# A gated mix of a long convolution and a token MLP on one core: filter transposed through 16-bit PSUM, more sums by accumulating transfers, gate scalings on ScalarE, the last tile cut 512 and 128, and a new fixed order

## The chip, the core and the metric

The kernel runs on one core of a Trainium2 chip. The metric is the device time of one execution in microseconds (us). In the text PE is TensorE, the matrix engine; PEld is its weight load, which overlaps the matmuls; DVE is VectorE; ACT is ScalarE; POOL is GpSimd; SP is SyncE, which here does nothing but issue transfers. SBUF is the on-chip memory, PSUM the accumulators that TensorE writes to.

## The reference

S = 2048 tokens, D = 640 channels, F = 1536. All inputs and the output are bf16. The random inputs are left out.

```python
def reference(A_q, A_k, A_v, A_shift_k, A_ssm_k, A_ssm_D, B_x, B_w1, B_b1, B_w2, B_b2, gate_w):
    def _A_ref(q, k, v, shift_k, ssm_k, ssm_D):
        ...
        for t in range(ks):                      # ks = 4
            k_shift = k_shift + k_pad[:, t:t + S, :] * shift_k[:, ks - 1 - t][None, None, :]
        kv = k_shift * v
        L = 2 * S
        ...
        y_f = kv_f * kf_f[None, :, :, :]         # rfft of kv and of ssm_k, both padded to L
        y = irfft(y_f)[:, 0, :S, :]
        y = y + kv * ssm_D[None, None, :]
        return q * y
    def _B_ref(x, w1, b1, w2, b2):
        h = _layernorm(x, axis=-1)
        u = jnp.einsum("bsd,sf->bdf", h, w1) + b1
        u = _gelu(u)
        y = jnp.einsum("bdf,fs->bds", u, w2) + b2
        return transpose(y, 0, 2, 1)
    x = A_q
    g = _sigmoid((x * gate_w).sum(-1, keepdims=True))
    a = _A_ref(x, A_k, A_v, A_shift_k, A_ssm_k, A_ssm_D)
    b = _B_ref(x, ...)
    return g * a + (1 - g) * b
```

The output is the gated sum of two branches over the same tokens: a causal convolution as long as the sequence (by a Fourier transform of length 4096), and an MLP that mixes tokens.

## The kernel before

**Branch A.** The Fourier transforms are matmuls with cosine and sine tables, after the sequence has been cut by residues of the token index (four parts `p`, two halves). `FE`, `FN` (made in the kernel with a Sin on ScalarE) and `FO` (loaded) are the forward tables, `GTB` the inverse ones. The filter `ssm` comes in as channels by tokens and has to be turned: `transp` does it with matmuls against an identity, eight of 128x128 for each of five channel blocks `db` and two halves, 80 in all; each eight fill one PSUM slot and are evicted to `wT` (L615 on ScalarE, L616 on VectorE). Before its matmuls `transp` adds `dcol`, a column of ssm_D, to the first column of each block on POOL. `wblock` transforms `wT` to the filter's spectrum W in `C[0]`, `C[1]`; `mixing` combines the parts on VectorE, in steps of 2560 or 5120 elements a partition. The keys `kn` are permuted to `kp` (`k_turn`, an operation that either ScalarE or VectorE does), turned by a transposing transfer to `KT`, and convolved with the four taps as matmuls (`kv`); ScalarE evicts to `ksh`, VectorE multiplies with v. `fwd` and `fwd_even` transform the result to `C[2]`, `C[3]`. `cross` and `product` multiply the spectra: `A0` and `A1` are the two halves of kv's spectrum, `V0` and `V1` those of the filter's. Some of the sums are not done by VectorE but by a transfer that adds to its destination, issued by POOL (L267, accum): so `late` in `product`, and `acc_dma`, which adds V1 to A1 in two transfers of 640 KB each for g = 1 and g = 0. `invmix` and `halved` prepare the inverse, `inverse` does its matmuls against `GTB`; ScalarE scales the result by the gate into `cgb`, VectorE multiplies by q (`q_hi`, `q_lo`: reloaded from the input late, since X's place is taken by then), and the product is added to `O1`, which already holds the MLP's result: for the first half h = 0 by an accumulating transfer, for h = 1 by VectorE.

**Branch B.** X holds the input, `ln_tile` takes mean and variance (two statistics operations of 320 and one that joins them, per tile of 128 tokens), `ln_scale` and `ln_apply` normalize in place. m1: 12 blocks `ft` of 32 matmuls with 320 columns, X against w1 (in `ring`), into one PSUM slot, then gelu on ScalarE into `GT`. m2: 16 tiles (hk, p) of 24 matmuls, GT against w2 (`W2`), evicted by ScalarE with scale and bias to `O1`; the last tile is evicted by two VectorE operations of 320 columns (`last_stt`, L627), which add the convolution's part.

**Gate.** gsum on ScalarE adds up q * gate_w per token; a few operations of 16 elements a partition on VectorE and a tanh make `gg` (g) and `omg` (1 - g).

**PSUM.** Four slots pp0 to pp3, each 128 x 1024 fp32 (two banks). Both branches take their slots from these four.

**The order.** Nothing is scheduled at run time. Every operation is recorded by `SC.add` with what it reads and writes; `follow` then takes a written list of the 649 operations (`_ORDER`), which fixes the order on every engine and every issuing queue, `_SLOTS` fixes the PSUM slot of each group, and `_ENG` the engine of each of the 50 operations that can run on either. `_Tracker` puts in the semaphore waits. Each engine works in the order of its list, so an instruction that waits holds up all behind it. Ahead of the first transposes TensorE runs matmuls on zeros (`spin`, tile `zz`, 512 columns each); they compute nothing. m1's and m2's matmuls stand between those of branch A, so that TensorE has work while VectorE is at the spectra.

In the profile the lines of helpers appear rather than their callers': L298 is every matmul, L556 every two-operand VectorE or POOL operation, L570 to L571 every operation with a scalar, L600 ScalarE's, L636 memsets, L615 and L616 the evictions on either engine, L267 POOL's and L272 SP's transfers.

Of the kernel before, what the change touches and what calls it, by code (L numbers as in the profile page):

```python
# [19 lines left out]
class _Tracker:  # L20
# [265 lines left out]
    def mm(self, ps_ap, lhsT, rhs, start, stop, final_val, inc, transpose=False):  # L286
# [11 lines left out]
        ins = self.nc.tensor.matmul(ps_ap, lhsT=lhsT, rhs=rhs, start=start, stop=stop, skip_group_check=True)  # L298
# [134 lines left out]
def _build(nc, A_q, A_k, A_v, A_shift_k, A_ssm_k, A_ssm_D, B_x, B_w1, B_b1, B_w2, B_b2, gate_w, out):  # L433
# [10 lines left out]
    with ExitStack() as es:  # L444
# [53 lines left out]
        cst = alloc("cst", [128, 2], F32)  # L498
# [27 lines left out]
        ksh = [alloc(f"ksh{i}", [128, 4, D], BF16, at=base_of(GT) + 5120 * (1 + i)) for i in range(2)]  # L526
        rows = alloc("rows", [20, 5, 512], BF16, at=base_of(GT))
# [110 lines left out]
        def mms(vt, items, prio=None, name="mm"):  # L638
            dur = sum(max(n_of(r) / 2400.0 + 0.0025, 0.056) for _, _, r, _, _ in items)
            rd = []  # L640
            for _, l, r, _, _ in items:
                rd += [l, r]

            def emit(s):
                fv = T.cnt["PE"] + 1
                for k_, (o, l, r, st, sp) in enumerate(items):
                    T.mm(o(s), l, r, st, sp, fv, k_ == len(items) - 1)
            return SC.add("PE", dur, emit, rd, [], prio=prio, vt=vt, name=name)
# [43 lines left out]

        def x_load(hk):
            dma(X[:, hk, :, :], qrow(hk), 128 * 5120, chain=True, rate=(352.0 if hk == 0 else 415.0))
# [28 lines left out]
        ssm_load(0, 0, 1)  # L723
        for a, b in ((0, 1), (1, 4)):
            dma(X[:, 0, a:b, :], dr(A_q, a * D, [[4 * D, 128], [1, (b - a) * D]]), 128 * 1280 * (b - a), chain=True)
        ssm_load(1, 0, 1)
        for db in range(1, ND):
# [3 lines left out]
        for hk in range(1, 4):  # L731
            x_load(hk)
# [14 lines left out]
        memset("DVE", cst[:, 1:2], -0.5)  # L747
        iota = lambda ap, pat, b, cm: nolock("POOL", 0.1 + n_of(ap) / 1100.0, lambda s: T.op("POOL", lambda e: e.iota(ap, pat, base=b, channel_multiplier=cm), [], [ap]), [], [ap])
# [49 lines left out]
        def transp(h, db):  # L798
# [5 lines left out]
            for j in range(7, -1, -1):  # L804
                items.append(((lambda s, j=j: s[:, 128 * j:128 * j + 128]), V(ssm, db * S + 1024 * h + j, [[8, 128]]), ident[:, :], True, True))
            m_ = mms(vt, items, name="wtr")
            evac("wT", V(wT, 2 * h * SL + 128 * db, [[SL, 2], [D, 4], [1, 128]]), (lambda s: s[:, :].rearrange("q (a b c) -> q a b c", a=2, b=4)), vt, 1.0 / 1024.0)
# [93 lines left out]

        def ln_scale(a, b):
# [24 lines left out]
        for h in range(2):  # L927
# [5 lines left out]
            if h == 0:  # L933
# [20 lines left out]
                def stats_of(k):  # L954
                    for t in range(LB[k], LB[k + 1]):
                        b0, b1, ag = ln_tile(t // 4, t % 4)
# [19 lines left out]
                mixing(C[0], SS, 0, fine=True, prio=MIXP)  # L976
# [104 lines left out]
        ts("DVE", gpre[:, :], mv[:, :, 0], gws[:, 0:1], None, ALU.mult, mode=1)  # L1081
        tt("DVE", gpre[:, :], gpre[:, :], gth[:, :], ALU.add, mode=1, prio=0)
        act(gth[:, :], gpre[:, :], ACT.Tanh, scale=0.5, prio=0)
        ts("DVE", gg[:, :], gth[:, :], 0.5, 0.5, ALU.mult, ALU.add, mode=1, prio=0)
        ts("DVE", omg[:, :], gth[:, :], -0.5, 0.5, ALU.mult, ALU.add, mode=1, prio=0)
# [20 lines left out]

        INVP = ((0, 2, 1, 3), (1, 3, 0, 2))
        for hk, p in [(hk, p) for hk in range(2) for p in range(4)] + [(hk, p) for p in INVP[1] for hk in (2, 3)]:
# [7 lines left out]
            for a in range(na):  # L1116
                items = []
                for ft, ci in order[a * (24 // na):(a + 1) * (24 // na)]:
                    items.append((chk(ci), w2t(hk, p, ft), GT[:, ft, 320 * ci:320 * ci + 320], ft == 0, ft == FT - 1))
# [26 lines left out]
        def product(dst, a, v, late=None, into=None):  # L1146
# [14 lines left out]
            tt("DVE", P2(T1), P2(a), P2(v, True), ALU.mult)  # L1161
            tt("DVE", H(dst, 0), H(T0, 0), H(T0, 1), ALU.subtract)
            tt("DVE", H(dst, 1), H(T1, 0), H(T1, 1), ALU.add)
# [32 lines left out]
        def invmix(Ya, Yb, sc, bfirst=False, behind=None):  # L1196
# [8 lines left out]
            for (hy, sy), k in (((hb, sb), 1), ((ha, sa), 0)) if bfirst else (((ha, sa), 0), ((hb, sb), 1)):  # L1205
# [29 lines left out]
        def inverse(h, Z, G=None):  # L1235
            for p in INVP[h]:
# [24 lines left out]
                tt("DVE", qv if h == 0 else cg[:, :, :], cg[:, :, :], qv, ALU.mult)  # L1261
                if h == 1 and p == INVP[1][-1]:
# [4 lines left out]
                    for ci in range(2):  # L1267
                        last_stt(O1[:, 3, p, 320 * ci:320 * ci + 320], chk(ci), omg[:, t:t + 1], cg[:, 1, 320 * ci:320 * ci + 320], lastvt[ci])
                    dma(rows_of(1, p, 1, 1), O1[:, 3, p, :], 128 * 1280, sem="out")
                elif h == 0:  # L1270
                    dma(ov, qv, 128 * 2560, stream="POOL", prio=0, accum=True)
                    dma(rows_of(0, p, 0, 2), ov, 256 * 1280, sem="out")
# [19 lines left out]
        chained(product, A1[1], A1[1], V0[1], tmp_of(q_hi, 0), V1[1])  # L1292
        chained(product, A1[0], A1[0], V0[0], tmp_of(q_hi, 1), V1[0])
        acc_dma(A1[1], V1[1])
        acc_dma(A1[0], V1[0])
        chained(product, A0[1], A0[1], V0[1], H(V0[1], 0))
        lastacc = SC.ops[-1]
        assert lastacc.eng == "POOL"
        for kt in range(2):
            dma(q_hi[:, kt, :, :], qrow(kt), 128 * 5120, wait=[H(A0[1], 1)]).deps.add(lastacc)  # L1300
        chained(product, A0[0], A0[0], V0[0])
        for kt in range(2):
            dma(q_lo[:, kt, :, :], qrow(2 + kt), 128 * 5120)
# [15 lines left out]
13 1 24 20 26 41 6 0 55 23 29 31 28 21 2 30 32 25 22 7 53 27 51 33 10 34 11 57 35 14 42 36 59 17 37 8 52 56 12 39 40 4  # L1319
48 44 142 54 136 9 49 50 145 43 135 203 3 67 233 137 5 139 68 204 60 138 58 144 61 18 69 141 209 74 140 62 182 75 210  # L1320
207 146 76 65 208 183 143 79 160 66 166 163 72 80 156 81 157 147 211 184 73 159 162 82 161 158 212 164 124 95 63 118
96 123 83 181 215 165 70 120 64 117 100 84 216 167 119 148 121 213 107 85 187 150 205 71 104 188 151 114 88 89 168 122
101 206 169 77 115 102 103 90 86 125 116 185 126 214 91 105 98 171 127 97 87 186 219 106 99 108 92 172 174 93 129 78
109 220 110 221 178 197 222 94 149 130 217 112 236 113 198 19 133 225 179 237 218 131 45 223 267 191 111 235 226 46
199 224 155 128 201 132 170 134 200 192 382 202 255 234 176 153 173 264 177 256 387 189 265 262 152 240 260 154 190
241 383 263 242 388 175 193 261 389 180 194 243 257 384 258 266 253 390 254 196 274 244 391 272 385 238 259 275 239
273 366 386 195 268 247 270 269 367 246 227 271 278 280 279 282 368 281 283 276 284 316 277 245 47 228 313 317 311 314
318 312 309 319 285 320 369 286 310 321 301 230 370 287 297 302 299 288 229 289 300 295 290 322 293 249 296 401 298
250 315 294 291 329 292 327 231 402 330 328 333 325 232 334 331 403 332 326 303 252 323 335 337 336 404 251 338 348
324 372 405 340 38 341 373 397 342 371 339 398 346 16 304 343 374 347 344 349 352 345 356 353 452 377 375 357 354 400  # L1330
376 306 406 380 381 350 305 399 15 421 379 351 307 422 378 355 423 308 424 392 407 360 395 416 425 408 358 396 361 393
417 533 394 359 418 411 419 459 461 538 409 415 420 446 460 532 412 447 414 413 448 426 441 442 535 428 458 248 430
443 534 410 436 429 537 427 536 449 444 431 539 432 451 363 541 437 453 438 540 454 450 445 474 456 457 362 433 455
# [36 lines left out]
```

## Time and profile before

| what | value |
|---|---|
| median of 3 runs | 177.09 us (176.99 to 177.10) |
| the profiled execution | 177.12 us |
| its span, first to last instruction | 175.1 us |
| mean granted TensorE clock | 1.00 |
| moved by transfers | 44.06 MB, mean 252 GB/s |

Where each engine is busy over the span shows in 40 equal slices (a digit is the busy share in tenths, 9 means 90% or more; PEclk is the granted clock; DMA the share of the 16 transfer engines):

```profile
PE   7999999999899999999999999999999999999992
PEld 2599999877697767777777778888899998698782
DVE  7899999999999999999999999999999999999984
ACT  4499999997999997877556214222215105645760
POOL 3199891000000650003202202220055000052200
PEclk9999999999999999999999999999999999999999
DMA  5999999999999799992999999999939999549598
```

The costliest groups of instructions (busy time, mean ns of one, idle time before them and what ended it) that the change touches:

```profile
L556 DVE TENSOR_TENSOR C<-C 128x2560 bf16<-128x2560 bf16 (+2 forms) x38 | 54.6, 1485 | 0.3 <-ACT C L600 0.2
...
L267 POOL DMA_DIRECT2D C<-C x8 | 10.5, 1674 | 51.1 <-DVE C L556 30.0
...
L600 ACT ACTIVATE gq<-gq 128x640 bf16<-128x640 bf16 x16 | 11.6, 727 | 5.7 <-DVE gq L556 5.7
L556 DVE TENSOR_TENSOR tm<-C,C 128x5120 bf16<-128x5120 bf16 x5 | 14.1, 2819 | 0.1
L897 DVE BATCH_NORM_STATS2 stats<-X 128x6 f32<-128x320 bf16 x32 | 13.1, 470 | 0.4 <-DMA X<-in_A_q_dram 0.2
```

A group's busy time is not its price. Each VectorE product of 2560 lasts 1.48 us but the next starts 1.40 us after it, and a matmul of 320 columns lasts 299 ns while the next starts 136 ns after it: times from start to start add up, durations don't.

### The profile page before, as it was taken

The page shows a single profiled execution, that of the slowest core. Times are in us where ns is not written, and L with a number is a line of the kernel's source. Part 1 is how long each engine was busy: PE and PEld are TensorE (multiplying, and loading weights), DVE is VectorE, ACT ScalarE, POOL GpSimd, SP SyncE. Part 2 cuts the span into 40 slices and gives each one's busy share as a digit, 9 for nine tenths or more (in the row PEclk, how much of TensorE's full clock was granted, in tenths as well). Part 3 has the DMA queues.
Part 4 walks back from the last instruction along what each step waited for, and adds up shares of the span by engine and source line. Part 5 has one row for each costly group of instructions (what it writes and reads, how often), then busy time and mean ns, then how long its engine had stood idle before and what let it go on. Part 6 is the DMA issues. An engine that isn't in the chain of part 4 may idle for free.

```text
span 175.1 us, 3683 instructions
## 1 busy us (share of the span) xinstructions
PE 170.0 (97%) x1559; PEld 138.2 (79%) x1559; DVE 168.9 (96%) x187; ACT 107.6 (61%) x160; POOL 42.7 (24%) x62
## 2 busy tenths in 40 slices
PE   7999999999899999999999999999999999999992
PEld 2599999877697767777777778888899998698782
DVE  7899999999999999999999999999999999999984
ACT  4499999997999997877556214222215105645760
POOL 3199891000000650003202202220055000052200
PEclk9999999999999999999999999999999999999999
DMA  5999999999999799992999999999939999549598
GB/s 144 397 421 405 376 200 225 380 375 221 179 383 356 172 192 192 186 358 57 178 174 365 353 211 349 282 207 240 300 108 187 197 177 372 241 65 209 106 233 292
DMA packets 33248, 44.06 MB, mean 252 GB/s; under 512 B 12112, under 2 KB 24656, under 8 KB 33104
## 3 DMA queue, kind: packets, MB, share of 16 engines
q1 hardware_dynamic: 28024, 32.68, 57.6%
q0 software_dynamic: 5168, 11.14, 37.4%
q8 instruction: 12, 0.20, 0.4%
q14 instruction: 4, 0.03, 0.1%
q10 hardware_dynamic: 40, 0.01, 0.0%
HBM read 27.44 MB, written 2.62 MB: 172 GB/s over the span
## 4 chain that ended last, share of the span: by engine, by line
PE 93%; DMA 3%; ACT 2%; DVE 0%; DVEq 0%; SPq 0%; issue 0%
PE pp L298 93%; DMA ssm<-in_A_ssm_k_dram 3%; ACT L600 1%; ACT ksh L600 1%; ACT GT L600 0%; DVE O L627 0%; DVEq L426 0%; SPq L272 0%
## 5 line engine op out<-in xcount | busy, mean ns | idle before, releaser
L298 PE MATMUL pp<-X,ring 128*128 128x320 bf16 x384 | 55.4, 299 | 0.5 <-ACT GT L600 0.5
L556 DVE TENSOR_TENSOR C<-C 128x2560 bf16<-128x2560 bf16 (+2 forms) x38 | 54.6, 1485 | 0.3 <-ACT C L600 0.2
L298 PE MATMUL pp<-GT,W 128*128 128x320 bf16 x384 | 53.6, 299 | 0.0
L298 PEld LDWEIGHTS pp<-GT,W 128*128 128x128 bf16 x384 | 48.0, 129 | 4.6
L298 PEld LDWEIGHTS pp<-X,ring 128*128 128x128 bf16 x384 | 37.0, 98 | 15.0 <-ACT GT L600 0.8
L600 ACT ACTIVATE O<-pp,c,omg 128x640 bf16<-128x640 f32 x15 | 12.9, 883 | 24.8 <-PE pp L298 24.8
L267 POOL DMA_DIRECT2D C<-C x8 | 10.5, 1674 | 51.1 <-DVE C L556 30.0
L600 ACT ACTIVATE C<-pp 128x640 bf16<-128x640 f32 x32 | 20.4, 711 | 2.0 <-PE pp L298 2.0
L600 ACT ACTIVATE cgb<-pp,gg 128x640 bf16<-128x640 f32 x16 | 12.1, 795 | 13.3 <-PE pp L298 7.6
L615 ACT ACTIVATE C<-pp 128x1024 bf16<-128x1024 f32 x18 | 17.1, 1051 | 0.3 <-PE pp L298 0.3
L600 ACT ACTIVATE gq<-gq 128x640 bf16<-128x640 bf16 x16 | 11.6, 727 | 5.7 <-DVE gq L556 5.7
L556 DVE TENSOR_TENSOR tm<-C,C 128x5120 bf16<-128x5120 bf16 x5 | 14.1, 2819 | 0.1
L897 DVE BATCH_NORM_STATS2 stats<-X 128x6 f32<-128x320 bf16 x32 | 13.1, 470 | 0.4 <-DMA X<-in_A_q_dram 0.2
L298 PE MATMUL pp<-wT,FO 128*128 128x128 bf16 x160 | 12.4, 219 | 0.0
L600 ACT ACTIVATE GT<-pp,cc 128x640 bf16<-128x640 f32 x12 | 9.3, 793 | 4.8 <-PE pp L298 4.7
L298 PE MATMUL pp<-C,GTB 128*128 128x320 bf16 x80 | 11.9, 299 | 0.0
L298 PE MATMUL pp<-wT,FE 128*128 128x128 bf16 x120 | 11.7, 219 | 0.0
L556 DVE TENSOR_TENSOR SS<-C 128x2560 bf16<-128x2560 bf16 x8 | 11.7, 1482 | 0.0
L267 POOL DMA_DIRECT2D O<-q_hi x4 | 4.8, 1324 | 27.7 <-DVE q_hi L556 27.7
L600 ACT ACTIVATE ksh<-pp 128x1024 bf16<-128x1024 f32 (+1 forms) x12 | 10.1, 908 | 1.4 <-PE pp L298 1.3
L267 POOL DMA_DIRECT2D C<-q_hi x4 | 4.8, 1198 | 23.8 <-DVE q_hi L556 10.9
L556 DVE TENSOR_TENSOR C<-tm 128x2560 bf16<-128x2560 bf16 x7 | 10.3, 1487 | 0.1
(92 smaller groups left out, 225.3 us busy)
## 6 DMA issues: line engine op xcount, KB each, us to landing
ring<-in_B_w_dram SPq DMA_DIRECT2D x12, 512.0 KB, 8.8
W<-in_B_w_dram SPq DMA_DIRECT2D x12, 512.0 KB, 6.8
C<-C POOLq DMA_DIRECT2D x8, 640.0 KB, 8.8
kn<-in_A_k_dram SPq DMA_DIRECT2D x4, 640.0 KB, 9.6
C<-q_hi POOLq DMA_DIRECT2D x4, 640.0 KB, 9.7
out_dram<-O SPq DMA_DIRECT2D x7, 320.0 KB, 3.2
ssm<-in_A_ssm_k_dram SPq DMA_DIRECT2D x4, 512.0 KB, 7.0
X<-in_A_q_dram SPq DMA_DIRECT2D x3, 640.0 KB, 7.3
```

What stands on the lines that cost most here:

```text
L267: ins = engobj.dma_start(out_ap, in_ap, accum_op=ALU.add, max_dma_last_dim=2560)
L298: ins = self.nc.tensor.matmul(ps_ap, lhsT=lhsT, rhs=rhs, start=start, stop=stop, skip_group_check=True)
L556: o_ = SC.add(eng, d, lambda s: T.op(eng, lambda e: e.tensor_tensor(o, a, b, op), rd, [o]), rd, [o], prio=prio, name="tt")
L600: return T.op("ACT", lambda e: e.activation(o, src, func, **kw), rr + [src], ww)
L615: return either(name, o, i, [], lambda e, src: e.activation(o, src, ACT.Copy, **kw), lambda e, src: e.tensor_copy(o, src) if scale == 1.0 ...
L897: ops.append(SC.add("DVE", 0.38, (lambda o, i: lambda s: T.op("DVE", lambda e: e.bn_stats(o, i), [i], [o]))(o, i), [i], [o]))
```

## The change

- `T.mm` gets `is_transpose`; `transp` sets it and writes bf16 into PSUM, so that eight transposes fill half a slot. The evictions to `wT` read bf16.
- `cst` gets a fourth column that holds 0.5 (a memset on POOL). The gate's `gpre`, `omg` and `gg` are made by ScalarE instead of VectorE.
- The statistics of tile 11 are made by ScalarE (`ln_tile_act`: two passes over the tile with a running sum, and a tiny one between them).
- `mixing(C[0], ...)` takes its first steps 5120 wide, and `invmix` too where its two halves lie side by side.
- `product` loses the form with three operations on VectorE: both A0 products now add one part by an accumulating transfer. They come ahead of the A1 products, and each A1 product is followed by its own pair of `acc_dma`. The loads of `q_hi` lose a wait that held them until a sum had been issued.
- In `inverse` the second half's parts p = 1 and p = 3 are added to `O1` by an accumulating transfer instead of VectorE.
- The last m2 tile and its two evictions are cut at column 512 instead of 320; each piece has its own output transfer.
- Loads: block 4 of ssm and part 1 of X come first, in two pieces each (before, block 0 and part 0); FO, GTB and the small loads change places.
- `_ORDER`, `_SLOTS` and `_ENG` are new. In the new list the first 40 transposes stand back to back; all 14 matmuls on zeros are ahead of them (before, 12 ahead and two between). The 1.28 us load of ScalarE's gelu table stands behind the Sin at the start (before, ahead of the first gelu). 16 + 16 matmuls of m1 stand ahead of the first of `kv` (before 8 + 8). One of the four `kp` copies is on ScalarE, and seven wT evictions instead of eight.

```diff
-        ins = self.nc.tensor.matmul(ps_ap, lhsT=lhsT, rhs=rhs, start=start, stop=stop, skip_group_check=True)
+        ins = self.nc.tensor.matmul(ps_ap, lhsT=lhsT, rhs=rhs, start=start, stop=stop, skip_group_check=True, **({"is_transpose": True} if transpose else {}))
...
+        junk = alloc("junk", [128, D], BF16, at=base_of(GT) + 10240)
...
-        ssm_load(0, 0, 1)
+        ssm_load(0, 4, 5)
         for a, b in ((0, 1), (1, 4)):
-            dma(X[:, 0, a:b, :], dr(A_q, a * D, [[4 * D, 128], [1, (b - a) * D]]), 128 * 1280 * (b - a), chain=True)
-        ssm_load(1, 0, 1)
-        for db in range(1, ND):
+            dma(X[:, 1, a:b, :], xpart(1, a, b), 128 * 1280 * (b - a), chain=True)
+        ssm_load(1, 4, 5)
+        for db in [d for d in range(ND) if d != 4]:
...
+        memset("POOL", cst[:, NCST:NCST + 1], 0.5)
...
-                items.append(((lambda s, j=j: s[:, 128 * j:128 * j + 128]), V(ssm, db * S + 1024 * h + j, [[8, 128]]), ident[:, :], True, True))
-            m_ = mms(vt, items, name="wtr")
+                items.append(((lambda s, j=j: s[:, 64 * j:64 * j + 64].bitcast(BF16)), V(ssm, db * S + 1024 * h + j, [[8, 128]]), ident[:, :], True, True))
+            m_ = mms(vt, items, name="wtr", transpose=True)
...
+        def ln_tile_act(t):
+            xs = X[:, t // 4, t % 4, :]
+            r = 1.0 / math.sqrt(D)
+            act(junk[:, :], xs, ACT.Copy, scale=1.0 / D, acc=mv[:, t, 0:1], name="lnm")
+            act(cst[:, 2:3], mv[:, t, 0:1], ACT.Copy, scale=-r, name="lnb")
+            act(junk[:, :], xs, ACT.Square, scale=r, bias=cst[:, 2:3], acc=mv[:, t, 1:2], name="lnm")
...
-                mixing(C[0], SS, 0, fine=True, prio=MIXP)
+                mixing(C[0], SS, 0, prio=MIXP)
...
-        ts("DVE", gpre[:, :], mv[:, :, 0], gws[:, 0:1], None, ALU.mult, mode=1)
+        act(gpre[:, :], mv[:, :, 0], ACT.Copy, scale=gws[:, 0:1])
...
+        LASTC = (0, 512, 640)
...
-            tt("DVE", P2(T1), P2(a), P2(v, True), ALU.mult)
-            tt("DVE", H(dst, 0), H(T0, 0), H(T0, 1), ALU.subtract)
-            tt("DVE", H(dst, 1), H(T1, 0), H(T1, 1), ALU.add)
...
+            if ha is hb and sb + 2 == sa:
+                y0, y1 = (V(ha, (sb + j) * SL, [[2 * SL, 2], [1, SL]]) for j in range(2))
+                tt("DVE", V(hs, (ss + 1) * SL, [[-SL, 2], [1, SL]]), y0, y1, ALU.add)
+                tt("DVE", y0, y0, y1, ALU.subtract)
...
-                tt("DVE", qv if h == 0 else cg[:, :, :], cg[:, :, :], qv, ALU.mult)
+                by_dma = h == 0 or p in (1, 3)
+                tt("DVE", qv if by_dma else cg[:, :, :], cg[:, :, :], qv, ALU.mult)
...
-        chained(product, A1[1], A1[1], V0[1], tmp_of(q_hi, 0), V1[1])
-        chained(product, A1[0], A1[0], V0[0], tmp_of(q_hi, 1), V1[0])
-        acc_dma(A1[1], V1[1])
-        acc_dma(A1[0], V1[0])
-        chained(product, A0[1], A0[1], V0[1], H(V0[1], 0))
-        lastacc = SC.ops[-1]
-        assert lastacc.eng == "POOL"
-        for kt in range(2):
-            dma(q_hi[:, kt, :, :], qrow(kt), 128 * 5120, wait=[H(A0[1], 1)]).deps.add(lastacc)
-        chained(product, A0[0], A0[0], V0[0])
-        for kt in range(2):
-            dma(q_lo[:, kt, :, :], qrow(2 + kt), 128 * 5120)
+        for g in range(2):
+            chained(product, A0[g], A0[g], V0[g], tmp_of(tm[1], g))
+        for g in (1, 0):
+            chained(product, A1[g], A1[g], V0[g], tmp_of(q_hi, g), V1[g])
+            acc_dma(A1[g], V1[g])
+        for hk in range(2):
+            dma(q_hi[:, hk, :, :], qrow(hk), 128 * 5120)
+        for hk in range(2):
+            dma(q_lo[:, hk, :, :], qrow(2 + hk), 128 * 5120)
```

`_ORDER`, `_SLOTS` and `_ENG` are replaced as a whole and not shown.

## Prediction

> **What bounds the kernel now.** I read the busy shares and slices first, then the chain of waits, then the timeline at the chain's joints, then the transfers at the end.
>
> ```profile
> PE 170.0 (97%) x1559; PEld 138.2 (79%) x1559; DVE 168.9 (96%) x187; ACT 107.6 (61%) x160; POOL 42.7 (24%) x62
> ...
> PE 93%; DMA 3%; ACT 2%; DVE 0%; DVEq 0%; SPq 0%; issue 0%
> ```
>
> TensorE (PE) and VectorE (DVE) are both full. Being full is not yet being the bound; the chain in order of time says which one ends last:
>
> ```profile
> 1.19 5.37 DMA ssm<-in_A_ssm_k_dram
> 6.56 0.04 issue
> 6.60 27.17 PE pp L298 x443
> ...
> 41.09 1.02 ACT ksh L600
> 42.11 0.02 issue
> 42.13 1.28 ACT L600
> 43.41 0.01 issue
> 43.43 0.81 ACT GT L600
> 44.23 0.05 issue
> 44.28 127.63 PE pp L298 x988
> ...
> 171.93 0.55 DVE O L627
> 172.48 0.46 DVEq L426
> ```
>
> TensorE works from 6.60 to 171.91 and stops once for long: from 43.61, when the matmuls before it are done, until 44.28 it waits for the first gelu, which stood behind a 1.28 us reload of ScalarE's function table. All other idle places of TensorE after 6.60 come to about 0.6 us, and 0.43 us goes into two idle-spin matmuls on zeros at 7.65. So an edit that leaves the columns alone can gain some 1.2 to 1.7 us, no more. Two other resources are close behind:
>
> ```profile
> 15.00:20.00 5.00, 5.00 (x91) 5.00 (x89) 4.94 (x15) 5.00 (x8) 4.66 (x7) 1.00 1.03 405
> 20.00:25.00 5.00, 5.00 (x91) 4.97 (x90) 5.00 (x16) 5.00 (x7) 4.39 (x9) 1.00 1.26 246
> ```
>
> (busy PE, PEld, DVE, ACT, POOL of 5 us; clock; DMA share; GB/s.) ScalarE (ACT) has no room either from 15 to 25 us, and the DMA share is at 1.
>
> **The change, part by part.** The sum starts from the profiled execution, 177.12 us, of which 175.1 is its span and 2.0 lies around it; the median of the runs shown is 177.09, so the two agree.
>
> (a) *Head, to the first W matmul* (9.60 in before). The Pool engine (POOL) now makes three jrow tables (0.19 us each) ahead of brow, and memsets (0.36 for rows, 0.15 for m32) stand ahead of pint on DVE: pint ends 0.75 later and with it the 1.15 us Sin. Behind Sin ScalarE now does the table load (1.28) and a statistics pass over tile 11 (0.73, priced by a gsum row of the same 128x640), and only then dcol, for which the addition to ssm and so the transposes wait: 7.7 against 5.93, about 0.35 us of stall on TensorE after 6.6. A second pass (0.73), cw (0.28) and cc are ahead of the first wT eviction, so it ends at 10.07. Two spins fewer (0.43) give some of it back. First W matmul at 10.1: **+0.5**. If fillers hide it, 0; if each late step adds, +1.1.
>
> (b) *Table load gone from 42.13*: the gelu follows the ksh eviction at once. Its cover before was nothing, TensorE stood: **-0.67**.
>
> (c) *16-bit transposes.* The 80 matmuls keep their 128 columns (56 ns from start to start); I take no change. The evictions' bounds: on DVE 1.18, as now, to 0.43 (the row of an int16 1024-wide pass); on ScalarE 1.04 in both. Three of ten are on DVE, none is on TensorE's path once W runs: 0, range -0.3 to +0.3.
>
> The Trainium skill, "VectorE: DVE Perf Modes", section "Why PSUM operands drop a tier", says a PSUM operand in 16 bits may run at twice the rate that one in fp32 gets. By it the DVE eviction would be an estimated 0.6 us, and the sum would not change.
>
> (d) *ScalarE +3.3 us of work before 40 us*: a 128x2560 kp copy (2.4 by the slope of the 727 and 1051 ns rows, 2.9 by that to the 1149 one), two 0.73+0.19 passes, small ones; one eviction goes to DVE. Where ScalarE is full its followers, the slots' evictions, come later by up to that. The cover is the m1 filler matmuls put ahead of the k convolution, 32 x 0.136 = 4.35 us: 0 taken; without cover, up to +2. DVE loses 5.4 us (seven 2560-wide products at 1.40, three more 5120-wide at 2.74, two 1280-wide, three statistics, one kp copy, plus one eviction), mostly after 100 us, where TensorE is fed through other work: no gain by itself.
>
> (e) *The products and the accumulating transfers.* In before:
>
> ```profile
> 128.87 1.20 POOL L267 DMA_DIRECT2D C<-SS  x1 [10.41 <-DVE C L556]
> 129.60 4.17 POOL L267 DMA_DIRECT2D C<-C  x3
> ...
> 147.13 2.89 DVE L556 TENSOR_TENSOR SS<-C 128x2560 bf16<-128x2560 bf16 x2
> ...
> 164.12 4.51 PE L298 MATMUL pp<-SS,GTB 128*128 128x320 bf16 x32
> 168.47 3.42 PE L298 MATMUL pp<-GT,W 128*128 128x320 bf16 x24
> ```
>
> The four sums (issued 0.73 apart) land 6.2, 8.7, 11.3 and 14.9 us after issue by the rows of the transfers, so at 135.1, 138.3, 141.6 and 146.0: 3.2, 3.3 and 4.4 us apart. Afterwards the A0 products come first and the sums into A1 in two pairs. The first pair's DVE work ends where it does now, 128.9; the second follows one 5120-wide and four 2560-wide operations, 2.74 + 4 x 1.40, at 137.4. Ahead of and between them are two W loads (1.5 us each) and, no longer held back by a wait, two q_hi loads (1.7 each): 128.9 + 4 x 3.3 + 3.0 + 3.4 = 148.5 for the last landing. DVE waits for it with SS<-C, and behind that stand the rest of the inverse mixing and all that TensorE's last inverse needs: two 5120-wide and four 2560-wide, 11.5 us with the hand-overs. Then TensorE has 64 matmuls at 0.136 and the last tile, 12.2 with the start. So TensorE would end at 148.5 + 11.5 + 12.2 = 172.2, against 171.91 - 0.67 + 0.5 = 171.74 if nothing made it wait. The later decides; I take **172.1**, +0.2. The bounds: if the last lands as early as in before, 171.74 (-0.2); at 4.4 us for each of the four it is 172.2 + 4.4 = 176.6 (+4.7), but three of four in before were not so slow, so I value the step near its lower end.
>
> (f) *The end.* Twelve 512-wide matmuls (0.216) and twelve 128-wide (0.056) are 3.26 us, as 24 x 0.136 was. The last DVE operations, 128 and 512 wide, sum to the same 1.0 us. But two O1 sums of 320 KB go by transfer (4.1 us alone, by an O<-q_hi row), so one output of 320 KB starts at about 171 instead of before, and the outputs already land one per 0.92 us:
>
> ```profile
> out_dram<-O SPq DMA_DIRECT2D x1, 320.0 KB, 2.6
> out_dram<-O SPq DMA_DIRECT2D x1, 160.0 KB, 1.8
> ```
>
> Two of 320 KB and then 32 and 128 KB behind 172.1 are 2.3 us of backlog and 0.5 us of issue: the last lands near 175.2 instead of 174.8. **+0.2** on top of TensorE's end. If the sums land earlier, 0; if the backlog is whole, +0.8.
>
> (g) Load order, gate scalings (three tiny ones, 0.17 to 0.22 us each), the larger mixing steps: hidden behind TensorE's filler; exposed they cost up to 0.3.
>
> Sum: 177.12 + 0.2 (TensorE's end, which holds a to e) + 0.2 (f) = **177.5**. This kernel's measurement can tell some 0.2% (0.35 us) from no change.
>
> **The rivals.**
>
> *Faster.* The head's lateness is met by other matmuls and the sums land by 147 as now, for the q_hi loads are small and the two pairs compete less than four at once. For it: TensorE's slack in the filler stage, and that (b) is a stall surely removed. Against it: DMA share 1 and the longer way from the sums to the end. It gives -0.67 + 0.2 + 0 = 176.65, and with the two spins and half of the small gaps gone too, 176.1. It decides wherever the last sum lands before 148.
>
> *Sums late* (slower). The last sum takes 4.4 us, as the last in before, because loads share the engines: 149.6, and the end 173.3, 1.2 over what I took: 178.7; both of the second pair so slow, 179.8. For it: the fourth sum of before. Against it: the first three.
>
> *Transposes slow TensorE.* The change puts 40 transposes back to back, with no zero spins between, from 6.7 to about 10. If they do not keep the clock up, columns cost 0.427 us per 512 as in the first spins (ten took 4.30) in place of 0.216: 40 transposes from 2.24 to 4.5 us, +2.2: 179.7. For it: TensorE does start slow in before, ten spins at 0.43. Against it: the same 40 ran at 56 ns in before, with two spins of zeros among them.
>
> The Trainium skill, "TensorE: Matmul & The Clock Gate", section "Part 4: PE-mode transpose", says this mode does not count as TensorE being busy for the clock. Here the 80 were ordinary matmuls against an identity and become such ones, and no run of this case shows the mode yet; by the rule the time is this rival's.
>
> *It doesn't do what it says.* A 16-bit eviction takes as long as a 32-bit one. Then (c) is 0 exactly and 177.5 stays.
>
> **Chances.** Forecast, with its own range 176.9 to 178.1: 0.43, of which 0.14 falls within 0.2% (up to 177.44) and 0.29 above. Faster rival 0.34 (0.32 below 176.74, 0.02 within). Sums late 0.14, transposes 0.06, no effect of 16 bits 0.03 (within 0.01, above 0.02). That gives faster 0.32, same 0.17, slower 0.51. The range leaves out a tenth on each side: from 176.1, where the faster rival has everything, to 179.0, past the late sums.
>
> **What would show it.** First W matmul near 10.1, and dcol near 7.7 (a). A table load near 5.5 and none at 42; the gap at 43.6 gone (b). Transposes 56 ns apart at clock 1.00, DVE evictions from 16 bits below 1.18 (c). No TensorE idle time on ACT from 15 to 40 (d). The 5120-wide SS<-C waiting for a DMA until about 148.5, and TensorE waiting for DVE behind it (e): if TensorE shows no gap there, (e) is wrong and the time falls below 177. Outputs landing to 175.2 (f). A clock below 1 before 15 us, or TensorE gaps at the k convolution, would make the whole forecast wrong upward.

## The result, and the profile after

The changed kernel takes 186.83 us (median) against 177.04 us before: 1.0526 times as long, with a 95% interval of 1.0469 to 1.0584. One of its four executions, 189.61 us, fell in a slower state and is left out of the ratio, which compares the means of the others. The prediction was 177.5 us with a range up to 179.0. The sign was right, the size was not: 9.8 us were lost where 0.4 were forecast.

The profiled execution took 186.81 us with a span of 185.3. First the slices of its page, 40 equal parts of that span (4.6 us each), a digit being tenths of busy time and, for PEclk, tenths of TensorE's full clock:

```profile
PE   7999999999999609999999999999999999999990
...
PEclk9999999999999985899999999999999999999998
...
DMA  6999999999999999178589898998999998996796
```

In the 14th and 15th slice, from about 60 to 70 us, TensorE is idle, and for the two slices behind that its clock is down. The rest of TensorE's row looks as in the kernel before. The 20 us from 60 on held 150 matmuls in the kernel before and hold 83 now (before, then after: length, busy PE, PEld, DVE, ACT, POOL with instructions, granted clock, DMA share, GB/s):

```profile
60.00:80.00 20.00, 20.00 (x150) 14.25 (x148) 19.76 (x15) 16.12 (x31) 2.42 (x2) 1.00 1.06 227
```

```profile
60.00:80.00 20.00, 13.95 (x83) 8.87 (x82) 11.15 (x8) 9.18 (x16) 2.42 (x2) 0.83 0.83 174
```

The stretches of 20 us from 80 to 140 hold as many as before, 149 or 150 each. The loss is one event, not a slow-down of the whole. The waits of TensorE and the chain of work name it:

```profile
PE pp L298 <- DMA ring<-in_B_w_dram: 6.0, 1, 6.0
PE pp L298 <- DVE cst L638: 1.2, 1, 1.2
PE pp L298 <- DMA ssm<-in_A_ssm_k_dram: 0.2, 1, 0.2
```

```profile
50.16 0.55 SPq L272
50.71 0.04 issue
50.75 0.67 SPq L272
51.42 0.04 issue
51.47 17.73 DMA ring<-in_B_w_dram
69.19 0.04 issue
69.24 7.10 PE pp L298 x30
```

(In order of time: start, length, what.) TensorE waits once for 6.05 us, from 63.2 to 69.24, for the last of the four 512 KB pieces of w1 that go to the second ring buffer. SP issues this piece at 51.47 and it takes 17.73 us to land. What SP issued just ahead of it, and what landed late, stand in SP's timeline and in the list of transfers issued in that stretch (KB each, us to landing):

```profile
50.16 0.55 SPq L272 DMA_DIRECT2D ring<-in_B_w_dram  x1
50.75 0.67 SPq L272 DMA_DIRECT2D GTB<-inv_tab  x1
51.47 0.74 SPq L272 DMA_DIRECT2D ring<-in_B_w_dram  x1
...
GTB<-inv_tab SPq DMA_DIRECT2D x1, 1024.0 KB, 12.2
ring<-in_B_w_dram SPq DMA_DIRECT2D x1, 512.0 KB, 17.7
```

The 1 MB table GTB, needed for the first inverse at 149 us and not before, is now loaded ahead of a piece that TensorE needs at 63.2. In the kernel before, GTB was issued at 90.07, between the W loads, and the last ring piece landed 10.2 us after its issue:

```profile
ring<-in_B_w_dram SPq DMA_DIRECT2D x1, 512.0 KB, 10.2
```

GTB's own transfer is some 2.5 us: in the experiment below that holds the sums back, it lands 2.5 us behind the piece ahead of it (61.98 against 59.44). That alone would not make 17.7. The rest shows in the queues of the transfer engines, packets and share of 16 engines, in the windows 61 to 63 and 67 to 69 us. q1 carries SP's loads, q0 what POOL issues, here the first accumulating sums:

```profile
q0 software_dynamic: 121, 0.31, 81.1%
q1 hardware_dynamic: 171, 0.17, 28.3%
...
q0 software_dynamic: 171, 0.41, 108.2%
q1 hardware_dynamic: 13, 0.01, 2.2%
```

Two sums of 640 KB were issued at 56.62 and 57.62 and begin to move at about 60.5, when 363 of the ring piece's 512 packets of 1 KB are still to come. From then on the sums take most of the engines' time: between 67 and 69 us, 11 of the piece's packets go through (q1's other two have 4 bytes). Of the sixteen parts of the piece, one on each engine, the first has landed at 60.98, fourteen by 65.06, and the last two at 68.54 and 69.19.

The wait is not all that it costs. The windows before, in and behind it (busy PE, PEld, DVE, ACT, POOL with instructions, then the granted clock, DMA share, GB/s):

```profile
57.00:63.20 6.20, 6.19 (x46) 3.87 (x43) 6.20 (x5) 5.60 (x10) 4.56 (x4) 1.00 1.07 347
63.20:69.20 6.00, 0.00 (x0) 0.00 (x0) 5.05 (x3) 1.38 (x3) 0.16 (x1) 0.92 1.09 211
69.20:71.70 2.50, 2.46 (x10) 1.42 (x11) 0.00 (x0) 0.00 (x0) 0.00 (x0) 0.50 1.09 207
71.70:74.20 2.50, 2.50 (x11) 1.42 (x10) 0.00 (x0) 2.08 (x5) 0.00 (x0) 0.50 0.97 183
74.20:76.70 2.50, 2.50 (x17) 1.63 (x15) 0.00 (x0) 1.26 (x4) 0.00 (x0) 0.83 0.17 32
```

TensorE comes back at half its clock: 10 matmuls in 2.5 us instead of 18. PE's busy column is full there, so only the counts and the clock show it. The mean clock of the wait, 0.92, puts the fall to a half some 5 us into it, and the 0.83 of the last window puts the return at about 75.1. That is 5.8 us of work at half the clock, up to 2.9 us lost.

The Trainium skill, "TensorE: Matmul & The Clock Gate", section "HAM oscillation — how this bites in real kernels", describes this: a wait for a transfer longer than about 3.4 us takes TensorE's clock down to a half, and it starts again from there. The trace agrees: 6.05 us of standing still gave 0.50, and in an experiment below 1.66 us gave 1.00. Where between the two the limit lies, no run here shows.

### The profile page after: what moved, and what is told of

Its sections match the earlier page's. It is cut to its first block, busy times and chain, and to the rows that moved or that the text cites. A ratio compares the mean times of both kernels' runs of the same rounds, so it can differ in the third digit from the quotient of the medians.

```text
span 185.3 us, 3685 instructions
## 1 busy us (share of the span) xinstructions
PE 173.4 (94%) x1558; PEld 138.2 (75%) x1559; DVE 163.6 (88%) x175; ACT 111.6 (60%) x168; POOL 48.1 (26%) x66
## 4 chain that ended last, share of the span: by engine, by line
DVE 43%; DMA 21%; ACT 13%; PE 11%; SPq 6%; issue 3%; POOL 0%; DVEq 0%
DVE C L558 23%; PE pp L298 11%; DMA ring<-in_B_w_dram 10%; DVE tm L558 9%; DMA ssm<-in_A_ssm_k_dram 6%; SPq L272 6%; DMA C<-C 5%; ACT C L617 5%; DVE q_hi L558 3%; DVE SS L558 3%; DVE gq L558 3%; ACT ksh L602 3%; ACT X L930 2%; ACT kp L712 1%; ACT wT L617 1%
## 5 line engine op out<-in xcount | busy, mean ns | idle before, releaser
L298 PE MATMUL pp<-X,ring 128*128 128x320 bf16 x384 | 57.7, 307 | 6.0 <-DMA ring<-in_B_w_dram 6.0
L298 PEld LDWEIGHTS pp<-X,ring 128*128 128x128 bf16 x384 | 38.0, 100 | 21.9 <-DMA ring<-in_B_w_dram 6.4
L298 PE MATMUL pp<-GT,W 128*128 128x320 bf16 (+2 forms) x383 | 53.0, 299 | 0.1
L298 PEld LDWEIGHTS pp<-GT,W 128*128 128x128 bf16 x384 | 47.2, 129 | 5.4
L602 ACT ACTIVATE C<-pp 128x640 bf16<-128x640 f32 x32 | 21.0, 707 | 11.4 <-PE pp L298 9.7
L267 POOL DMA_DIRECT2D C<-C x8 | 9.9, 1415 | 67.2 <-DVE C L558 67.2
L602 ACT ACTIVATE gq<-gq 128x640 bf16<-128x640 bf16 x16 | 11.6, 724 | 11.5 <-DVE gq L558 11.5
L558 DVE TENSOR_TENSOR tm<-C,C 128x5120 bf16<-128x5120 bf16 (+1 forms) x5 | 12.7, 2553 | 0.0
L558 DVE TENSOR_TENSOR SS<-C 128x2560 bf16<-128x2560 bf16 (+1 forms) x6 | 11.4, 1931 | 0.2
L602 ACT ACTIVATE ksh<-pp 128x1024 bf16<-128x1024 f32 (+1 forms) x12 | 10.3, 914 | 0.5 <-PE pp L298 0.5
L298 PEld LDWEIGHTS pp<-C,GTB 128*128 128x128 bf16 x80 | 7.7, 98 | 3.0
L298 PEld LDWEIGHTS pp<-wT,FO 128*128 128x128 bf16 x160 | 9.8, 98 | 0.0
```

Of the source, the lines that this page charges most:

```text
L267: ins = engobj.dma_start(out_ap, in_ap, accum_op=ALU.add, max_dma_last_dim=2560)
L558: o_ = SC.add(eng, d, lambda s: T.op(eng, lambda e: e.tensor_tensor(o, a, b, op), rd, [o]), rd, [o], prio=prio, name="tt")
L602: return T.op("ACT", lambda e: e.activation(o, src, func, **kw), rr + [src], ww)
```

## The experiments

The theory (A): GTB's place on SP's queue put the last ring piece into the stretch in which the accumulating sums run, and these stretched it. Rival (B): the sums slow the piece wherever GTB stands. Rival (C): something else of the change is what counts. The edits to the order are moves of one number in the written list; operation numbers are those of the recorded list.

### GTB right behind the ring piece, and GTB where it was

```diff
 _ORDER (after; 247 is GTB, 246 the last ring piece)
-... 276 312 247 317 313 310 318 246 285 ...
+... 276 312 317 313 310 318 246 247 285 ...
```

> The changed kernel with one thing moved: the 1 MB GTB load stands right behind the last ring piece on SP's queue instead of right ahead of it. Theory A (GTB pushed the ring piece by 3.8 us, into the accumulating sums, which then stretched it): the piece lands near 61, before TensorE asks for it at 63.2, the 6.05 us wait and the half-speed stretch behind it are gone, and the time falls by about 8.7 us to 178.1. Rival B (the accumulating sums slow the piece wherever it stands): it lands at 65 or later, TensorE still waits 2 us or more, 181 or slower.

Measured: 178.20 us, ratio to the kernel before 1.0063 (1.0038 to 1.0089). The piece, by the list of transfers:

```profile
GTB<-inv_tab SPq DMA_DIRECT2D x1, 1024.0 KB, 12.9
ring<-in_B_w_dram SPq DMA_DIRECT2D x1, 512.0 KB, 10.4
```

It lands at 60.87, before it is needed, and TensorE no longer waits for it. 8.6 of the 9.8 us hang on the place of one load. B falls, for the sums are issued at nearly the same time as in the changed kernel (56.92 against 56.62); C falls for these 8.6 us.

```diff
 _ORDER (after)
-... 276 312 247 317 ... 533 458 435 ...
+... 276 312 317 ... 533 458 247 435 ...
```

> The changed kernel with the GTB load where the kernel before has it, between the W loads. Theory A: no wait for the ring, and the sums no longer share the engines with GTB either, 177.5 to 178.1 (what is left of the change beside the load order, forecast at 177.5). Rival B: 181 or slower, as in the run with GTB right behind the ring. If both runs end above 180 with no wait for the ring, something else in the change costs the time.

Measured: 179.99 us, ratio 1.0146 (1.0109 to 1.0182). No wait for the ring, but slower than with GTB behind the ring, which was not expected. The transfers give one reason: GTB now lands at 98.6, and the sums and W loads behind it land later (a q_hi sum issued at 90.04 takes 11.68 us, where it took 6.91; the C<-C sum issued about 97 takes 9.37 instead of 6.42). VectorE then waits 1.3 us for that sum, and TensorE, at the inverse transforms from 144 us on, waits three times for VectorE, 0.3 to 0.55 us each. These waits are 1.35 us, where the run with GTB behind the ring has 0.39. They are not the whole: in this profile, of the slowest of the four executions (180.95 us), TensorE ends 2.6 us later than there, and 1.0 of that are longer waits for the filter in the first 21 us, which GTB's place doesn't explain. In this order an early GTB is right in itself; it stood one place too early.

### GTB early in the kernel before

```diff
 _ORDER (before; 248 is GTB, 245 its last ring piece)
-... 284 316 277 245 47 228 ... 428 458 248 430 ...
+... 284 316 277 248 245 47 228 ... 428 458 430 ...
```

> The kernel before with one thing moved: GTB right ahead of its last ring piece. Theory A: that piece, needed at 60.3, lands at 63 or later, up to 69 if the sums stretch it; TensorE waits 3 to 9 us and then runs slow for a while: 181 to 187. Rival B (GTB is harmless, the sums decide): within 1 us of 177.04.

Measured: 178.50 us, ratio 1.0079 (1.0052 to 1.0106): slower, but not by the 4 to 10 us of the expectation. Its timeline and its clock:

```profile
61.86 1.26 PE L298 MATMUL pp<-X,ring 128*128 128x320 bf16 x8 [1.66 <-DMA ring<-in_B_w_dram]
```

```profile
61.80:64.30 2.50, 2.44 (x18) 1.78 (x19) 2.47 (x2) 0.87 (x2) 1.28 (x2) 1.00 1.08 203
```

The piece lands at 61.82 there, 11.0 us after its issue: GTB pushed it by some 2.5 us, but the sums, issued 0.8 us later than in the changed kernel (57.43), began to move at 60.69, when 22 of its 512 packets were left, against 363 in the changed kernel. So there GTB costs a wait of 1.66 us and no clock. The expensive part is the meeting with the sums, and about a microsecond decides whether they meet.

### The sums wait until the piece is there

```diff
-                    128 * 5120, stream="POOL", prio=0, accum=True)
+                    128 * 5120, stream="POOL", prio=0, accum=True, wait=[ring[1][:, 12:16, :]])
```

(in `v1mix` of the changed kernel, GTB left in its early place)

> The changed kernel, GTB where the change puts it, but the first four accumulating sums (C1<-C0, C0<-SS) are issued only when the last ring piece has landed. Theory A with both parts (queue place 3.8 us, stretch by the sums 4 to 5 us): the piece lands near 64.5 instead of 69.2, the wait shrinks from 6.05 to 1.3 us and with it the half-speed stretch: 180 to 181. If the queue place alone does it (no stretch by the sums): lands at 69, 186.8 unchanged. If the sums are then late for the cross products on VectorE (needed from about 83), 182 or more.

Measured: 179.56 us, ratio 1.0130 (1.0096 to 1.0164). The same piece, behind the same GTB:

```profile
ring<-in_B_w_dram SPq DMA_DIRECT2D x1, 512.0 KB, 11.6
```

It lands at 63.35 instead of 69.19, and TensorE's matmul follows at 63.40, 0.1 us late. This splits the delay: against 60.87 with GTB behind it, GTB's place is 2.5 us, of which TensorE felt 0.1; the sums are the other 5.8. In this kernel neither alone makes the wait. (The expectation had put GTB's place at 3.8 us and so a wait of 1.3.) What the run gives back elsewhere is in part the price of holding the sums back: the last of the four lands at 82.75 instead of 76.94, the next w1 pieces land behind them and keep TensorE waiting 0.24 us at 87, VectorE later waits 1.1 us for a sum, and TensorE twice for VectorE (0.31 and 0.42).

### The wait filled with work that computes nothing

```diff
+                if len(SC.ops) == 408:
+                    items = [((lambda s: pp[2][:, 0:320]), ident[:, :], X[:, 0, 0, 0:320], True, True)] * 44 + items
                 mms(vt, items, prio=10 ** 6 + 4 * ft + hk, name="m1")
```

(the changed kernel; operation 408 is the group that waits)

> The changed kernel with 44 matmuls that compute nothing (identity against X, 320 columns, into a slot that is free) put on TensorE ahead of the matmul that waits for the ring piece; the wait itself is untouched. If TensorE's slow stretch after the wait comes from having stood still, the matmuls behind it now run 136 ns apart and 2.5 us come back: about 184.3. If it has another cause (a limit on power, the transfers), the stretch stays and the time is 186.8.

Measured: 185.52 us, ratio 1.0458 (1.0398 to 1.0519). The windows of the wait and behind it:

```profile
64.50:71.20 6.70, 6.15 (x45) 4.23 (x45) 4.91 (x3) 1.22 (x3) 0.02 (x1) 1.00 1.09 211
71.20:73.70 2.50, 2.50 (x19) 1.82 (x20) 0.00 (x0) 0.93 (x2) 0.00 (x0) 1.00 1.09 206
```

19 matmuls in 2.5 us at clock 1.00, while the transfers are as busy as before (211 GB/s): standing still was what took the clock down, not the transfers. In this profile the piece came later still, at 71.15, so the time fell less than expected; but from the first matmul behind the wait to TensorE's end it is 109.04 us, and 111.75 in the changed kernel. The slow stretch costs 2.7 us.

### Smaller packets, the same bytes

```diff
+        elif out_ap.tensor.name.startswith("GTB"):
+            ins = engobj.dma_start(out_ap, in_ap, max_dma_last_dim=1024)
         else:
             ins = engobj.dma_start(out_ap, in_ap)
```

(in the kernel with GTB behind the ring piece)

> The changed kernel with GTB behind the ring piece, its 1 MB cut into packets of 1 KB, as w1's are, instead of 8 KB (64 per transfer engine instead of 8). It is under way when the accumulating sums start near 61, whose packets of 2.5 KB take 0.215 us each. If an engine serves the two queues packet by packet in turn, every small packet waits for one of the sums': 64 x (0.215 + 0.058) = 17.5 us, so GTB lands at 77 to 79 instead of 64.1 (nothing needs it before 135). If the engines share by bytes or by time, it lands by 67. The time of the kernel: 178.2 to 179, since the next w1 loads stand behind it.

Measured: 178.68 us, ratio 1.0091 (1.0067 to 1.0115). GTB's landing:

```profile
GTB<-inv_tab SPq DMA_DIRECT2D x1, 1024.0 KB, 18.8
```

It lands at 69.80 instead of 64.10. Neither number of the expectation was met: I had let all of its packets meet the sums, but some two thirds of them had gone through by 60.9. From then to 69.8 an engine that takes one 1 KB packet (0.05 to 0.06 us) for each of the sums' (0.215) moves some 33 of its 64. In the last two microseconds of that stretch the one engine still at it moved 8 packets of GTB while an engine does about 10 of the sums' on the average. So the direction is shown (the same bytes in smaller packets land 5.7 us later beside the sums; of this the smaller packets by themselves are some 0.5 us, an estimate from the ring pieces, whose 512 KB in 1 KB packets land 1.5 us apart, where GTB's 1 MB takes 2.5), and one-for-one service fits the counts; the trace does not name the engine of a packet, so it isn't proved.

The Trainium skill, "DMA: Bandwidth & Descriptors", section "Queues, rings and completion order", says that an engine serves its queues in turn, a packet at a time, and that a packet there is typically 9 to 17 descriptors. The later landing here fits service in turn; whether what the profile counts as packets are those of the page, no run here shows.

### The gelu table alone, and with other parts

```diff
 _ORDER (before; 36 is the Sin, 38 the table's dummy activation)
-... 14 42 36 59 17 ... 372 405 340 38 341 ...
+... 14 42 36 38 59 17 ... 372 405 340 341 ...
```

> The kernel before with one part of the change alone: ScalarE's gelu table is loaded right behind the Sin at the start instead of ahead of the first gelu. If TensorE's 0.67 us wait at 43.6 is the table load and nothing takes its place: 176.4. If something else ends that wait (the matmuls' slot, VectorE) or the head is delayed by the load: 177.0.

Measured: 176.41 us, ratio 0.9971 (0.9946 to 0.9996). This is the only run of the study whose interval lies below 1; the two runs that follow hold this edit too and don't repeat the gain. ScalarE's timeline has the load at the start, TensorE's has no hole at 43.6:

```profile
4.75 1.28 ACT L600 ACT_TABLE_LOAD   x1
...
42.38 2.34 PE L298 MATMUL pp<-X,ring 128*128 128x320 bf16 x16
```

```diff
-... 625 626 647 646 648
+... 625 626 646 647 648
```

(the same, and the last two VectorE operations in the order in which TensorE finishes their columns)

> The kernel before with the gelu table early, and its last two VectorE operations in the order in which TensorE finishes them (columns 0 to 319 first; until now both wait for TensorE's last matmul). The first can then start while TensorE does the last columns: 0.2 to 0.4 us less than with the table alone if the output transfers don't bind, so about 176.1. If the transfers ahead of the last one bind, no change against the table alone.

Measured: 177.08 us, ratio 0.9995 (0.9972 to 1.0019), where 176.1 to 176.4 was expected.

```diff
-        ins = self.nc.tensor.matmul(ps_ap, lhsT=lhsT, rhs=rhs, start=start, stop=stop, skip_group_check=True)
+        ins = self.nc.tensor.matmul(ps_ap, lhsT=lhsT, rhs=rhs, start=start, stop=stop, skip_group_check=True, **({"is_transpose": True} if transpose else {}))
...
-                items.append(((lambda s, j=j: s[:, 128 * j:128 * j + 128]), V(ssm, ...
+                items.append(((lambda s, j=j: s[:, 64 * j:64 * j + 64].bitcast(BF16)), V(ssm, ...
...
```

(the kernel before with the table early, and the transposes as in the change)

> The kernel before with the gelu table early and one more part of the change: the filter's transposes in transpose mode into 16-bit PSUM. As forecast in the prediction (c): the transposes keep 56 to 64 ns and clock 1.00, VectorE's two evictions fall from 1.18 to 0.69 us, ScalarE's eight from 1.04 to about 0.96, and the time stays that of the table alone, 176.4 (within 0.3). If the mode slows TensorE: 177.5 or more.

Measured: 177.25 us, ratio 1.0014 (0.9989 to 1.0040), where 176.4 was expected if the mode doesn't slow TensorE. It doesn't in this profile: the transposes last 227 ns each, as in the kernel before. VectorE's evictions fell to 691 ns; ScalarE's stayed at 1045. In both profiles, this one and the one before it, the hole at 43.6 is gone, and in both another has come in its place. The waits of the last one:

```profile
PE pp L298 <- DVE zz L636: 1.2, 1, 1.2
PE pp L298 <- DMA KT<-kp: 0.8, 1, 0.8
PE pp L298 <- DMA ssm<-in_A_ssm_k_dram: 0.4, 1, 0.4
```

TensorE, 0.7 us earlier now, stands at 48.7 before the second turned half of the keys, whose last part lands at 49.81 (49.74 in the run with the final operations exchanged, 47.25 with the table alone). So in these three profiles the table's 0.67 us is won only where that transfer lands early. Why it does so in some executions is open. The profile with the table alone is of the fastest of its eleven executions (176.10 us), the other two are of the slowest of theirs (177.86 and 177.85), so they don't tell how often either happens. Neither of the two edits shows an effect of its own: the last output follows TensorE's end by 2.9 us whichever of the final operations comes first, and the eviction from 16 bits is off TensorE's path.

### Repairing the rest of the change

With GTB behind the ring piece, the sums of parts 1 and 3 back on VectorE:

```diff
-                by_dma = h == 0 or p in (1, 3)
+                by_dma = h == 0
```

> The changed kernel with GTB behind the ring piece, and in addition the sums into O1 of the second half's parts 1 and 3 on VectorE again, as in the kernel before, instead of by accumulating transfers. In the run with GTB behind the ring the last output landed 3.7 us after TensorE's end, in the kernel before 2.9. If the two late sums and the outputs queued behind them make this, 0.5 to 0.8 us come back: 177.4 to 177.7. If the outputs are late for another reason, or VectorE's two additions delay the last ones as much, 178.2.

Measured: 177.96 us, ratio 1.0039 (1.0014 to 1.0064). The last output follows TensorE's end by 2.8 us instead of 3.7, so the tail is repaired; the time fell by 0.24 us only, less than the 0.5 to 0.8 expected, while single executions differ by more (eight of the eleven took 176.8 to 178.6, three 179.5 to 180.4). So the later landing is explained, its worth in time not settled.

In addition, the load of b1 on ScalarE's queue:

```diff
-        small(rows[0:12, 2, 0:128], dr(B_b1, ...), 3072, "SP", chain=True)
+        small(rows[0:12, 2, 0:128], dr(B_b1, ...), 3072, "QA", chain=True)
```

> The changed kernel with GTB behind the ring piece, the late sums on VectorE, and the small load of b1 (1.3 us into SP's queue ahead of the filter) issued by ScalarE's queue instead of SP's. If the filter's loads set the head of the changed kernel (first W matmul at 10.4 to 10.6 in the experiments, 9.6 in the kernel before), they come 0.48 us earlier and the time falls to 177.5 from 177.96. If ScalarE's work sets it: 177.96 unchanged.

Measured: 176.70 us, ratio 0.9996 (0.9968 to 1.0024). TensorE no longer waits for the filter in its profile, and the first W matmul starts at 10.04 instead of 10.3 to 10.6 as in the six variants above that have b1 on SP's queue. But the changed kernel itself has 9.92 with b1 on that queue, so the profile leaves open how much of this is the edit. The time fell by 1.26 us where 0.46 was expected; the head is 0.26 of it, and for the rest no cause is shown. And last, the final two operations exchanged:

```diff
-... 633 646 644 647 645
+... 633 644 646 645 647
```

> The changed kernel with its three repairs (GTB behind the ring piece, the late sums on VectorE, the b1 load on ScalarE's queue: 176.7 in the run before) and the last two VectorE operations in the order in which TensorE finishes them, the 512 columns first. They start during TensorE's last twelve 128-wide matmuls (0.67 us): 0.3 to 0.5 us less, 176.2 to 176.4, if the last output is what ends the kernel; no change, 176.7, if the outputs queued ahead of it are.

Measured: 177.03 us, ratio 0.9993 (0.9971 to 1.0014). No gain: the last output is issued 0.37 us earlier than in the run before (172.49 against 172.86) and lands at the same time (174.53 against 174.56), so the outputs queued ahead set the end. Repaired in three places, the change is worth nothing either way that these runs can tell.

## Why the prediction was wrong, step by step

**The step that failed is (g).** It read: "Load order, gate scalings (...), the larger mixing steps: hidden behind TensorE's filler; exposed they cost up to 0.3." The load order cost 8.6 us: 6.05 of wait and some 2.7 of half clock. The prediction put it at nothing without a row to show it, and the rows were there. Its list of the change has GTB changing places, and it priced every sum on POOL's queue for the products at 130 us, but did not ask which load is under way when the *first* four sums start at 57, nor when TensorE needs the piece that GTB pushes. The trace of before shows the last ring piece landing at 59.28, one microsecond ahead of its first use at 60.30, and the sums' packets starting at 59. A push of 2.5 us had nowhere to go. That the sign came out right owes nothing to the sum as far as these 8.6 us go. With the load order put right the change is still 1.1 us slower than the kernel before (178.20 against 177.10), where 0.4 was forecast.

**None of the rivals named it.** They were about a faster end, the late sums of the products, the transposes and the 16-bit evictions. The last line of the prediction's tests does not cover it either: it looked for gaps at the k convolution.

With GTB behind the ring piece the rest of the change can be read as it was forecast: 178.20 us where 177.5 was said, inside the range and just above the forecast's own 176.9 to 178.1.

- (a) Head. Forecast: first W matmul at 10.1, dcol at 7.7, +0.5. The changed kernel has 9.92 and 7.41, six of its variants 10.3 to 10.6. The size is about right; the cause was not ScalarE, whose dcol is done by 7.6 in all of them. In the six, TensorE waits 0.2 to 1.3 us for the filter's loads, whose third piece lands at 9.2 to 9.5. With b1 on ScalarE's queue that piece lands at 8.8, but so it does in the changed kernel itself, so that the b1 load ahead of it is the cause is likely and not shown.
- (b) Table. Forecast -0.67; alone it gave 0.55 (176.41 against 176.96 in the same runs), and the hole is gone in every kernel that loads it early. Right as to the wait. What it is worth depends on the keys' transfer, which keeps TensorE waiting 0.8 to 0.9 us in the other two runs with the table early (177.08 and 177.25).
- (c) Transposes. Right: 0. The groups by shape, before and after:

```profile
L616 DVE TENSOR_SCALAR wT<-pp 128x1024 bf16<-128x1024 f32 x2 | 2.4, 1182 | 0.0
L615 ACT ACTIVATE wT<-pp 128x1024 bf16<-128x1024 f32 x8 | 8.1, 1042 | 1.1 <-PE pp L298 1.1
```

```profile
L618 DVE TENSOR_SCALAR wT<-pp 128x1024 bf16<-128x1024 bf16 x3 | 2.1, 692 | 1.0 <-PE pp L298 1.0
L617 ACT ACTIVATE wT<-pp 128x1024 bf16<-128x1024 bf16 x7 | 7.0, 1032 | 0.3 <-PE pp L298 0.3
```

  VectorE's eviction fell from 1182 to 692 ns, within the bounds given; ScalarE's stayed (1042 before). The rival "it doesn't do what it says" falls for VectorE and holds for ScalarE. The rival of the slow transposes falls: 40 in a row at clock 1.00, at 227 ns each as before. From start to start they are 63 ns apart in both kernels (24 from 8.08 to 9.60 before, 40 from 7.38 to 9.92 after), not the 56 ns that (c) took; this changes nothing in the sum.
- (d) ScalarE. Right: TensorE has no wait on it from 15 to 60 us.
- (e) The products. Right, closely, though the working's 128.9 + 2.74 + 4 x 1.40 is 137.2 and not 137.4. With GTB behind the ring piece the second pair of sums is issued at 137.81 (forecast 137.4), the last lands at 148.88 (148.5), TensorE ends at 172.5 (172.1), and it feels the chain by this much:

```profile
160.60 4.25 PE L298 MATMUL pp<-SS,GTB 128*128 128x320 bf16 x30 [0.39 <-DVE SS L558]
```

- (f) The end. Mis-sized: the last output lands 3.7 us after TensorE's end (2.9 in before), so +0.8, the upper bound given, and not the +0.2 taken.

The profiled execution with GTB behind the ring took 178.34 us, 0.8 more than forecast. TensorE ends 0.4 later than was taken, and the last output follows it 0.6 later (3.7 us where 175.2 - 172.1 = 3.1 was taken). From that landing to the end of the execution it is 2.1 us where the kernel before has 2.3; this was not forecast and has no cause here.

## What to carry to other kernels

When a load moves on a queue, follow the load that it pushes: when does it land now, when is it needed, and what starts on another queue in between. Here the slack was one microsecond and the load moved ahead took 2.5; because a second queue with larger packets started in that moment, the delay was 8.3 us (69.19 against 60.87), three times the transfer's own time. A stall of TensorE that is long enough to take its clock down costs its length and then some, here 6.05 and 2.7 us; cost both.

## What the runs showed of the hardware that was not expected

- A load of 512 KB in 1 KB packets that alone lands 11.6 us after issue (behind 1 MB) took 17.7 beside accumulating sums with 2.5 KB packets of 0.215 us; 1 MB in 8 KB packets beside the same sums lost little (landing 3.2 us behind the piece ahead of it, 2.5 without the sums), in 1 KB packets 5.7 us more.
- Some 5 us into a wait of 6.05 us without a matmul TensorE's granted clock fell to a half, and 5.8 us of the work behind the wait ran at it; after 1.66 us it kept 1.00; dummy matmuls in the wait kept 1.00.
- An eviction from 16-bit PSUM instead of 32-bit takes 692 instead of 1182 ns on VectorE, and no less on ScalarE (1032 against 1042).
